# The order of the Strassen slots of the first feed-forward network, on TensorE, ScalarE and VectorE

## The chip, the cores and the metric

One core of a Trainium2 chip runs the whole program in one launch. The metric is the device time of that core in microseconds; the kernel before takes 1050.8 us (median of three runs, 1050.67 to 1052.14). TensorE multiplies, ScalarE (ACT) applies functions and copies, VectorE (DVE) and GpSimd (POOL) do elementwise work, SyncE (SP) issues most DMAs.

## The reference

A channel attention over 6016 tokens of 256 channels is followed by two feed-forward networks (256 to 2048 to 256), in float32:

```python
x = attn_out.reshape(B * S, D)
h = x @ w_in;   x = (h * np.cos(h)) @ w_out                 # first network ("FFN 1")
h = x @ w_in2;  x = (h * (1 / (1 + np.exp(-h)))) @ w_out2   # second ("FFN 2")
```

The kernel folds the attention matrix into the first network's weights, so that this network's input is v.

## The kernel before

The 6016 tokens are cut into 12 blocks: 11 of 512 columns and a last ("plain") one of 384. Each block passes the 2048 hidden features in eight steps of two times 128 (`NPAIR`). One such pair of one block is a *slot*. Every float32 operand is kept as a high and a low part (`hi`, a rounded copy, and `lo`, the remainder), and each product is three matmuls (`PASSES`): high by high, low weight by high, high by low.

From block 3 on, the first layer of FFN 1 is formed by seven Strassen products P1 to P7 on quarter blocks (`product`, L974; 256 columns each) instead of eight plain ones. Blocks 3 to 10 make 64 such slots, numbered 0 to 7 here within a block by the pair; the plain block's eight follow, and then FFN 2 with 88 Strassen slots of its own.

`first_layer` (L1325) writes out one step of a software pipeline by hand; each engine runs its instructions in the order in which this function issues them. Step j works on three units: u (slot j, whose products begin), p (slot j-1, whose products end, and whose cosines are taken) and q (slot j-2, whose result enters the output matmuls). For u, P1 goes into x2 (`xz[k2][:, 1]`), P7 on z2 (`xz[k2][:, 0]`); ScalarE copies z2 aside (`p7s`, L1346) and x2 into y2 (`ys[k2][:, 1]`, L1350); P2 is added onto x2, P6 onto y2, and y2 is copied aside as u2 (L1403). One step later, for p: P4 is added onto z and VectorE adds u2 (L1335; the addition itself is in `add`, L1028); P5 onto y, and VectorE adds the P7 copy into `ys[k][:, 0]` (L1361); P3 onto y. Then `xz` and `ys` hold the four quarters of the hidden block. Each of the two goes through a sine on ScalarE (L1348 for xz, L1386 for ys; a cosine by its bias), a multiply of the two on VectorE (L1362, L1390), the high part on ScalarE (L1374 "hi1", L1391 "hi0") and the low part on VectorE (L1375 "lo1", L1400 "lo0"). The 12 output matmuls of 512 columns (`o1_of`, L1304, matmul at L1315) run as 2, 6 and 4 between the products.

Beside this chain the slots carry *side work* for later stages, placed by the slot's number in `misc_act`, `misc_dve` and `misc_late` (L1233 to L1262):
- the next block's V: four GpSimd subtractions ("V forms"), its high parts on ScalarE (L923, L927) and low parts on GpSimd (L916), in slots 1, 2, 3; the reduction of its largest values on VectorE (L401) in slot 3; its bound, two small matmuls and two small VectorE steps, in slot 7;
- the decoding of FFN 2's weights in phases: a ScalarE copy (L313) with a GpSimd step (L290) in slots 5 and 7, two VectorE "clamps" (L296, L297) in slots 6 and 0, a VectorE sign step (L303) with GpSimd's L306 and combine (L355) in slots 7 and 1, and the split, a ScalarE copy (L358) with two GpSimd subtractions (L360), in slots 0 and 3;
- x2, the previous block's input to FFN 2 (`begin_x2`, L826): three copies out of the outputs in slot 4, the forms on VectorE (L858, L861) and GpSimd (L862), high parts on ScalarE (L848) and low parts on GpSimd (L853) in slots 5, 6, 7, each low followed by two stores on SP's queue.

In the kernel before, all of a slot's side work stands between the P7 copy and hi1 in program order. A slot ends with

```python
            product(y2, "P6", w_, x_, start=False)      # L1396
            nc.scalar.activation(u2, y2, AF.Copy)       # L1403
```

## Time and profile before

| | |
|---|---|
| median of 3 runs | 1050.8 us |
| the profiled execution's own time | 1052.19 us |
| its span, first to last instruction | 1050.3 us |
| TensorE busy | 1006.4 us (96%) |
| VectorE busy | 857.5 us (82%) |
| ScalarE busy | 796.7 us (76%) |
| GpSimd busy | 371.7 us (35%) |
| granted TensorE clock, mean | 0.999 |
| idle of TensorE before the outputs' L1315, put down to hi0 (L1391) | 17.0 us |

Busy time is the share in which an engine has an instruction running; matmuls are pipelined and their recorded lengths overlap the next ones' starts, so a TensorE that reads as busy need not be issuing as fast as it can. The chain that ended last gives 57% of the span to TensorE, 18% to ScalarE and 14% to VectorE. Times in rows are microseconds from the start of the span; L numbers are lines of the kernel before.

### The profile page before, as it was taken

To read this page: it belongs to the slowest core of one execution; us is meant where nothing else is said; L and a number is where in the kernel's file an instruction comes from. 1 tells how busy PE (TensorE), PEld (TensorE's weight loads), DVE (VectorE), ACT (ScalarE), POOL (GpSimd) and SP (SyncE) were. 2 spreads that over 40 slices of the span, in tenths; PEclk is the share of its full clock that TensorE was granted. 3 is DMA by queue.
4 is the path that set the end of the run, shared out by engine and by line. 5 is a ranking of instruction groups with operands and counts; after the bars stand their busy time and mean duration, and the time that the engine had idled before them with its cause. 6 is when DMAs were issued, how large, how long until landed. Compare 5 with 4: busy or idle time off the path is not lost.

```text
span 1050.3 us, 18664 instructions
## 1 busy us (share of the span) xinstructions
PE 1006.4 (96%) x7062; PEld 935.5 (89%) x7062; DVE 857.5 (82%) x1295; ACT 796.7 (76%) x1453; POOL 371.7 (35%) x367
## 2 busy tenths in 40 slices
PE   9999999999999898999989999999999999999998
PEld 8767888888888787888878999999999999999997
DVE  6799889777767777777877589999999999999972
ACT  6786676677777777777777688888878888888863
POOL 4433388526456464646435311111111111111110
PEclk9999999999999999999999999999999999999999
DMA  9940036422333333243336971202211220220101
GB/s 349 347 154 1 1 139 239 163 90 106 126 120 131 111 121 131 81 151 116 129 132 244 413 290 71 91 11 82 91 57 46 81 91 12 81 91 12 56 22 38
DMA packets 35012, 126.59 MB, mean 121 GB/s; under 512 B 3170, under 2 KB 4450, under 8 KB 30178
## 3 DMA queue, kind: packets, MB, share of 16 engines
q1 hardware_dynamic: 34770, 125.12, 32.2%
q8 instruction: 57, 0.93, 0.4%
q14 instruction: 41, 0.34, 0.1%
q10 hardware_dynamic: 144, 0.20, 0.1%
HBM read 73.01 MB, written 52.30 MB: 119 GB/s over the span
## 4 chain that ended last, share of the span: by engine, by line
PE 57%; ACT 18%; DVE 14%; issue 7%; DMA 2%; POOL 1%; SPq 0%; DVEq 0%; ACTq 0%; POOLq 0%
PE o L978 19%; PE xz L978 12%; PE ys L978 9%; PE o L766 6%; DVE ys L1390 4%; PE h L734 3%; ACT hi L1391 3%; ACT t L1348 3%; ACT hi L1374 3%; DVE xz L1028 3%; ACT t L1386 2%; DVE lo L1375 2%; ACT ys L1350 2%; DMA qk<-qk_dram 2%; PE o L1018 1%
## 5 line engine op out<-in xcount | busy, mean ns | idle before, releaser
L796 DVE TENSOR_TENSOR lo<-t,hi 128x768 fp32r<-128x768 f32 (+1 forms) x176 | 194.8, 1116 | 28.7 <-ACT hi L788 28.5
L783 POOL TENSOR_TENSOR t<-t 128x256 f32<-128x256 f32 x88 | 64.5, 733 | 356.7 <-DVE t L780 296.7
L788 ACT ACTIVATE hi<-t 128x768 fp32r<-128x768 f32 (+1 forms) x176 | 169.1, 961 | 27.2 <-PE o L978 26.2
L1315 PE MATMUL o<-hi,wo 128*128 128x512 f32 x512 | 137.4, 391 | 18.0 <-ACT hi L1391 17.0
L978 PE MATMUL o<-hi,wo 128*128 128x256 f32 x770 | 134.6, 275 | 0.0
L1315 PEld LDWEIGHTS o<-hi,wo 128*128 128x128 f32 x512 | 87.0, 189 | 35.6 <-ACT hi L1391 28.8
L978 PEld LDWEIGHTS o<-hi,wo 128*128 128x128 f32 x770 | 116.9, 192 | 0.0
L978 PE MATMUL o<-lo,wo 128*128 128x256 f32 x385 | 105.9, 275 | 0.0
L978 PE MATMUL xz<-xhi,wa 128*128 128x256 f32 x384 | 77.8, 288 | 12.5 <-DVE lo L1375 10.3
L1391 ACT ACTIVATE hi<-ys 128x512 fp32r<-128x512 f32 x64 | 38.2, 597 | 57.1 <-DVE ys L1390 57.1
L978 PEld LDWEIGHTS xz<-xhi,wa 128*128 128x128 f32 x384 | 62.6, 190 | 20.6 <-DVE lo L1375 12.5
L1400 DVE TENSOR_TENSOR lo<-ys,hi 128x512 fp32r<-128x512 f32 x64 | 44.3, 692 | 40.3 <-ACT hi L1391 40.3
L978 PE MATMUL ys<-xhi,wf 128*128 128x256 f32 x384 | 74.0, 274 | 0.5 <-DVE ys L1028 0.5
L978 PEld LDWEIGHTS ys<-xhi,wf 128*128 128x128 f32 x384 | 67.7, 190 | 7.5 <-DVE ys L1028 0.7
L978 PEld LDWEIGHTS o<-lo,wo 128*128 128x128 f32 x385 | 73.9, 192 | 0.0
L1348 ACT ACTIVATE t<-xz,half_pi,smalls 128x512 f32<-128x512 f32 x64 | 49.8, 778 | 31.3 <-DVE xz L1028 30.9
L1467 ACT ACTIVATE ys<-xz 128x256 f32<-128x256 f32 x88 | 32.4, 368 | 45.4 <-PE xz L978 44.5
L1315 PE MATMUL o<-lo,wo 128*128 128x512 f32 x256 | 65.9, 380 | 0.0
L978 PE MATMUL xz<-x2hi,wf 128*128 128x256 f32 x352 | 65.8, 275 | 0.0
L978 PE MATMUL xz<-x2hi,wa 128*128 128x256 f32 x352 | 65.8, 275 | 0.0
L766 PE MATMUL o<-hi,wo 128*128 128x512 f32 (+1 forms) x256 | 62.7, 367 | 1.4 <-POOL wo L351 1.4
L1375 DVE TENSOR_TENSOR lo<-xz,hi 128x512 fp32r<-128x512 f32 x64 | 44.1, 689 | 24.4 <-ACT hi L1374 23.7
(271 smaller groups left out, 3176.8 us busy)
## 6 DMA issues: line engine op xcount, KB each, us to landing
qk<-qk_dram SPq DMA_DIRECT2D x22, 512.0 KB, 7.6
x2hi<-xshi SPq DMA_DIRECT2D x11, 896.0 KB, 5.3
x2lo<-xslo SPq DMA_DIRECT2D x11, 896.0 KB, 7.2
wi_dram<-stage SPq DMA_DIRECT2D x8, 1024.0 KB, 4.4
wo_dram<-stage SPq DMA_DIRECT2D x8, 1024.0 KB, 4.7
vraw<-vT_dram SPq DMA_DIRECT2D x11, 512.0 KB, 5.8
outT_dram<-q SPq DMA_DIRECT2D x22, 256.0 KB, 2.0
xshi<-t SPq DMA_DIRECT2D x10, 512.0 KB, 2.6
```

The source lines that it names most:

```text
L766: nc.tensor.matmul(o[:, e, :n], wo1_at(i, f)[:, e * P : (e + 1) * P], columns(parts[k][:, s, :n]), start=(f == 0 and (i, k) == PASSES[0]), ...
L783: eng.tensor_tensor(out=t[:, 7, :c], in0=t[:, 3, :c], in1=t[:, 6, :c], op=ALU.subtract)
L788: nc.scalar.activation(hi[:, sl, :c], t[:, 1:][:, sl, :c], AF.Copy)
L796: nc.vector.tensor_tensor(out=lo[:, sl, :c], in0=t[:, 1:][:, sl, :c], in1=hi[:, sl, :c].bitcast(F32), op=ALU.subtract)
L978: nc.tensor.matmul(out, w(p, ka), columns(x[r][:, kb - 1]), start=(start and i == 0), stop=(stop and i == 2), skip_group_check=True,)
L1315: nc.tensor.matmul(o[:, e], wo1_at(i, f)[:, e * P : (e + 1) * P], columns(parts[k][:, s]), start=(f == 0 and (i, k) == PASSES[0]), stop=(f ...
L1348: nc.scalar.activation(sines[:, 1], xz[k], AF.Sin, bias=half_pi, scale=small[p[1]])
L1375: nc.vector.tensor_tensor(out=ls[:, 1], in0=xz[k], in1=hs[:, 1].bitcast(F32), op=ALU.subtract)
L1390: nc.vector.tensor_tensor(out=ys[k], in0=ys[k], in1=sines[:, 0], op=ALU.mult)
L1391: nc.scalar.activation(hs[:, 0], ys[k], AF.Copy)
L1400: nc.vector.tensor_tensor(out=ls[:, 0], in0=ys[k], in1=hs[:, 0].bitcast(F32), op=ALU.subtract)
L1467: nc.scalar.activation(y2, x2, AF.Copy)
```

## The change

The slot keeps its products, copies, sines, multiplies and parts; their order and the place of the side work are others.
- TensorE: P4 and P5 of p come first, then P1 and P7 of u, then P3 between two pairs of output matmuls, P6 in mid slot, and P2 last, behind the remaining four pairs. Outputs run from separate lists of high and low passes, two matmuls at a time.
- ScalarE: the y2 copy first, then the two sines one after the other, the P7 copy, hi1, hi0, u2; `misc_act` follows u2.
- VectorE: the two additions, `misc_dve`, the two multiplies, lo1, lo0, then the bound and `misc_late`.
- One buffer for the P7 copy (`seeds[0]`) where two took turns; x2's third seed is always `seeds[2]`.
- x2's steps are the same four for every block: the raw low parts now stand a slot later than the raw high parts.
- When the last Strassen slot's outputs meet the plain block, they are spread over two steps (`halved`).

```diff
@@ -828,8 +828,6 @@
         if b == PLAIN:
             return begin_x2_plain(b)
         c, t, t0 = HB, Y, seeds[2]
-        if FIRST <= b < PLAIN - 1:
-            t0 = plain_part(T[1])[:, :HB]
         src = [state[1, b][:, a].rearrange("p (b h j) -> p j h b", h=2, j=2) for a in range(CH)]
         nc.scalar.activation(t[:, 1:3].rearrange("p j (h b) -> p j h b", h=2), src[1], AF.Copy)
         nc.scalar.activation(t0.rearrange("p (h b) -> p h b", h=2), src[0][:, 0], AF.Copy)
@@ -867,17 +865,10 @@
                 lambda: (low("raw", RAW), high("formed", FORMED)),
                 lambda: low("formed", FORMED),
             ]
-        if b < 2:
-            return [
-                lambda: forms(nc.vector, eng),
-                lambda: high("raw", RAW),
-                lambda: (low("raw", RAW), high("formed", FORMED)),
-                lambda: low("formed", FORMED),
-            ]
         return [
             lambda: forms(nc.vector, eng),
-            lambda: (high("raw", RAW), low("raw", RAW)),
-            lambda: high("formed", FORMED),
+            lambda: high("raw", RAW),
+            lambda: (low("raw", RAW), high("formed", FORMED)),
             lambda: low("formed", FORMED),
         ]
 
@@ -1239,6 +1230,8 @@
             xsteps[1]()
         if m in (6, 7):
             xsteps[m - 4]()
+        if m == 7:
+            xsteps.clear()
         decode_steps(b, m, "act")
         if b + 1 < PLAIN:
             if m == 1:
@@ -1252,8 +1245,6 @@
         decode_steps(b, m, "dve")
         if m == 5:
             xsteps[0]()
-        if m == 7:
-            xsteps.clear()
         if b + 1 == PLAIN and m == 2:
             vs.pop(0)()
 
@@ -1306,10 +1297,11 @@
         if (1, b) not in state:
             state[1, b] = ps_o.tile([P, CH, TB], F32, tag="o", name=f"o1_{b}")
         o = state[1, b]
-        todo = [(s, r, e) for r in PASSES for s in range(2) for e in range(CH)]
-
-        def run(count):
-            for _ in range(count):
+        high = [(s, r, e) for r in PASSES[:2] for s in range(2) for e in range(CH)]
+        low = [(s, PASSES[2], e) for s in range(2) for e in range(CH)]
+
+        def run(todo):
+            for _ in range(CH):
                 s, (i, k), e = todo.pop(0)
                 f = 2 * m + s
                 nc.tensor.matmul(
@@ -1318,20 +1310,30 @@
                     columns(parts[k][:, s]),
                     start=(f == 0 and (i, k) == PASSES[0]),
                     stop=(f == NF - 1 and (i, k) == PASSES[-1]),
+                    skip_group_check=True,
                 )
 
-        return run
+        return lambda: run(high), lambda: run(low)
+
+    halved = []
 
     def first_layer(j, u, p, q, o):
         k, k2 = (j - 1) % 2, j % 2
         up, pp_, qp, op_ = [v is not None and v[1] == PLAIN for v in (u, p, q, o)]
         ps, qs = p is not None and not pp_, q is not None and not qp
-        p7s, u2 = seeds[::2], seeds[1]
+        p7, u2 = seeds[:2]
+        o_high = o_low = lambda: None
+        if qs:
+            o_high, o_low = o1_of(q[1:], hl.pop(j - 2))
+        if qs and pp_:
+            halved.extend([o_high, o_high, o_high, o_high, o_low, o_low])
+            o_high = o_low = lambda: None
         if ps:
             w, x = w1_slot(p[2]), xparts[p[:2]]
             y, z = ys[k][:, 1], xz[k][:, 0]
             sines, hs, ls = [parted(r) for r in (T[0], HI[k], LO[k])]
             product(z, "P4", w, x, start=False)
+            product(y, "P5", w, x, start=False)
             add(z, z, u2)
         if j < 2:
             open_quadrants(j)
@@ -1343,64 +1345,61 @@
             y2, x2, z2 = ys[k2][:, 1], xz[k2][:, 1], xz[k2][:, 0]
             product(x2, "P1", w_, x_, start=True)
             product(z2, "P7", w_, x_, start=False)
-            nc.scalar.activation(p7s[k2], z2, AF.Copy)
+        if ps:
+            add(ys[k][:, 0], y, p7)
+        if not up:
+            misc_dve(u[1], u[2])
+            nc.scalar.activation(y2, x2, AF.Copy)
+        o_high()
         if ps:
             nc.scalar.activation(sines[:, 1], xz[k], AF.Sin, bias=half_pi, scale=small[p[1]])
+            product(y, "P3", w, x, start=False)
+            nc.scalar.activation(sines[:, 0], ys[k], AF.Sin, bias=half_pi, scale=small[p[1]])
         if not up:
-            nc.scalar.activation(y2, x2, AF.Copy)
+            nc.scalar.activation(p7, z2, AF.Copy)
+        if ps:
+            nc.vector.tensor_tensor(out=xz[k], in0=xz[k], in1=sines[:, 1], op=ALU.mult)
+            nc.scalar.activation(hs[:, 1], xz[k], AF.Copy)
+            nc.vector.tensor_tensor(out=ys[k], in0=ys[k], in1=sines[:, 0], op=ALU.mult)
+            nc.scalar.activation(hs[:, 0], ys[k], AF.Copy)
+            for i, r in ((1, xz[k]), (0, ys[k])):
+                nc.vector.tensor_tensor(out=ls[:, i], in0=r, in1=hs[:, i].bitcast(F32), op=ALU.subtract)
+            hl[j - 1] = [flat(r[k]) for r in (HI, LO)]
         if j < 2:
             step()
         if j == 0:
             parts[pend] = emit_split(pend, units[pend])
         while left and (j == 1 or len(left) > 2):
             emit_left()
-        if qs and not qp:
-            hl.setdefault(("run", j - 2), o1_of(q[1:], hl.pop(j - 2)))(2)
-        if ps:
-            product(y, "P5", w, x, start=False)
-            add(ys[k][:, 0], y, p7s[k])
-            nc.vector.tensor_tensor(out=xz[k], in0=xz[k], in1=sines[:, 1], op=ALU.mult)
+        o_high()
+        if not up:
+            product(y2, "P6", w_, x_, start=False)
+        o_low()
+        o_high()
+        o_high()
+        o_low()
         if pp_:
             plain_cosines(j - 1, p)
         if qp:
             high_and_low(j - 2, q, True)
         if up:
             tail_of_first(j)
-        else:
-            misc_act(u[1], u[2])
-            misc_dve(u[1], u[2])
-            misc_late(u[1], u[2])
-        if ps:
-            nc.scalar.activation(hs[:, 1], xz[k], AF.Copy)
-            nc.vector.tensor_tensor(out=ls[:, 1], in0=xz[k], in1=hs[:, 1].bitcast(F32), op=ALU.subtract)
         if qp:
             high_and_low(j - 2, q, False)
-        if qs:
-            hl["run", j - 2](6 if ps else 4)
+        if halved:
+            for _ in range(3):
+                halved.pop(0)()
         elif op_:
             emit_o1(o[1:], hl.pop(j - LAG2))
-        elif ("run", j - LAG2) in hl:
-            hl.pop(("run", j - LAG2))(6)
-        if ps:
-            product(y, "P3", w, x, start=False)
-            nc.scalar.activation(sines[:, 0], ys[k], AF.Sin, bias=half_pi, scale=small[p[1]])
-        if qs and ps:
-            hl.pop(("run", j - 2))(4)
-        if ps:
-            nc.vector.tensor_tensor(out=ys[k], in0=ys[k], in1=sines[:, 0], op=ALU.mult)
-            nc.scalar.activation(hs[:, 0], ys[k], AF.Copy)
         if up:
             emit_plain_h1(u[1:], 1, bank(ys[k2], BLOCKS[PLAIN][1]))
         else:
+            nc.scalar.activation(u2, y2, AF.Copy)
             product(x2, "P2", w_, x_, start=False)
-            product(y2, "P6", w_, x_, start=False)
             if u[2] == NPAIR - 1:
                 bound(u[1] + 1, xz[k][:, 0])
-        if ps:
-            nc.vector.tensor_tensor(out=ls[:, 0], in0=ys[k], in1=hs[:, 0].bitcast(F32), op=ALU.subtract)
-            hl[j - 1] = [flat(r[k]) for r in (HI, LO)]
-        if not up:
-            nc.scalar.activation(u2, y2, AF.Copy)
+            misc_act(u[1], u[2])
+            misc_late(u[1], u[2])
 
     def tail_of_first(j):
         nonlocal q_sums, late
```

How this moves instructions: a middle slot on TensorE, before (xz_1463 and ys_1462 belong to p, xz_1423 to u; wa and wf are weights, o the outputs):

```order
L978 MATMUL xz_1463<-xhi_1152,wa_90 128x256 x2
L978 MATMUL xz_1463<-xlo_1153,wa_90 128x256
L978 MATMUL xz_1423<-xhi_1152,wa_91 128x256 x2
L978 MATMUL xz_1423<-xlo_1153,wa_91 128x256
L978 MATMUL xz_1423<-xhi_1152,wf_1049 128x256 x2
L978 MATMUL xz_1423<-xlo_1153,wf_1049 128x256
L1315 MATMUL o_3_1528<-hi_502,wo_1_94 128x512 x2
L978 MATMUL ys_1462<-xhi_1152,wf_1048 128x256 x2
L978 MATMUL ys_1462<-xlo_1153,wf_1048 128x256
L1315 MATMUL o_3_1528<-hi_502,wo_1_94 128x512 x6
L978 MATMUL ys_1462<-xhi_1152,wf_1048 128x256 x2
L978 MATMUL ys_1462<-xlo_1153,wf_1048 128x256
```

and in the change (xz_1466 and ys_1465 belong to p, xz_1423 and ys_1422 to u):

```order
L969 MATMUL xz_1466<-xhi_1152,wa_90 128x256 x2
L969 MATMUL xz_1466<-xlo_1153,wa_90 128x256
L969 MATMUL ys_1465<-xhi_1152,wf_1048 128x256 x2
L969 MATMUL ys_1465<-xlo_1153,wf_1048 128x256
L969 MATMUL xz_1423<-xhi_1152,wa_91 128x256 x2
L969 MATMUL xz_1423<-xlo_1153,wa_91 128x256
L969 MATMUL xz_1423<-xhi_1152,wf_1049 128x256 x2
L969 MATMUL xz_1423<-xlo_1153,wf_1049 128x256
L1307 MATMUL o_3_1515<-hi_502,wo_1_94 128x512 x2
L969 MATMUL ys_1465<-xhi_1152,wf_1048 128x256 x2
L969 MATMUL ys_1465<-xlo_1153,wf_1048 128x256
L1307 MATMUL o_3_1515<-hi_502,wo_1_94 128x512 x2
```

P5 (the first two rows of ys before) has moved up to the place behind P4, ahead of P1 and P7, and only two output matmuls stand ahead of P3.

ScalarE in slot 2 of a block, before (spare and p are the two P7 copies, t the sines, u is u2):

```order
L1346 ACTIVATE p_1053<-xz_1423 128x256
L1348 ACTIVATE t_500<-xz_1463,half_pi,smalls 128x2x256
L1350 ACTIVATE ys_1422<-xz_1423 128x256
L927 ACTIVATE xhi_2794<-vform_2796 128x1024
L1374 ACTIVATE hi_503<-xz_1463 128x2x256
L1386 ACTIVATE t_500<-ys_1462,half_pi,smalls 128x2x256
L1391 ACTIVATE hi_503<-ys_1462 128x2x256
L1403 ACTIVATE u_1054<-ys_1422 128x256
```

and in the change:

```order
L1352 ACTIVATE ys_1422<-xz_1423 128x256
L1355 ACTIVATE t_500<-xz_1466,half_pi,smalls 128x2x256
L1357 ACTIVATE t_500<-ys_1465,half_pi,smalls 128x2x256
L1359 ACTIVATE p_1053<-xz_1423 128x256
L1362 ACTIVATE hi_503<-xz_1466 128x2x256
L1364 ACTIVATE hi_503<-ys_1465 128x2x256
L1397 ACTIVATE u_1054<-ys_1422 128x256
L918 ACTIVATE xhi_2828<-vform_2830 128x1024
```

The copy xhi<-vform, side work of slot 2, stood ahead of the high parts hi and now stands behind u2, ahead of the next slot's y2 copy; the sines t stand together.

GpSimd in slots 0 to 2 of a block, before (stage is the split, vform the V forms, xlo V's low part):

```order
L360 TENSOR_TENSOR stage<-wv_wi_2575,stage 128x512 x2
L916 TENSOR_TENSOR vform_2796<-vraw_2518 128x256 x2
L916 TENSOR_TENSOR vform_2796<-vraw_2518,vform_2796 128x256 x2
L306 TENSOR_TENSOR wv_wi_2680<-wv_wi_2680,raw_wi_2366 128x512
L355 TENSOR_TENSOR wv_wi_2680<-wv_wi_2680 128x128 x4
L916 TENSOR_TENSOR xlo_2795<-vraw_2518,xhi_2794 128x768
```

and in the change:

```order
L360 TENSOR_TENSOR stage<-wv_wi_2601,stage 128x512 x2
L306 TENSOR_TENSOR wv_wi_2718<-wv_wi_2718,raw_wi_2352 128x512
L355 TENSOR_TENSOR wv_wi_2718<-wv_wi_2718 128x128 x4
L907 TENSOR_TENSOR vform_2830<-vraw_2544 128x256 x2
L907 TENSOR_TENSOR vform_2830<-vraw_2544,vform_2830 128x256 x2
L907 TENSOR_TENSOR xlo_2829<-vraw_2544,xhi_2828 128x768
```

The sign step and combine of slot 1 (wv_wi, L306 and L355) have moved ahead of the four V forms.

## Rows read from the trace of the kernel before

**Rows 1.** Stretch of FFN 1's slots, busy us: PE, PEld, DVE, ACT, POOL; clock, DMA.
```profile
350.00:400.00 50.00, 45.79 (x288) 40.91 (x288) 37.60 (x63) 37.97 (x73) 28.76 (x30) 1.00 0.31 111
```

**Rows 2.** Line L1403, u2's copy, one a slot: durations, first and last start.
```profile
L1403 ACT ACTIVATE u<-ys x64: 378/379/383, 194.6 to 562.5; 128x256 f32<-128x256 f32 x64
```

**Rows 3.** Line L1512, the same copy in FFN 2's Strassen slots.
```profile
L1512 ACT ACTIVATE u<-ys x88: 380/406/428, 597.5 to 1005.3; 128x256 f32<-128x256 f32 x88
```

**Rows 4.** Timeline, TensorE, block 6: start, length, instruction, count, idle before, releaser.
```profile
364.57 0.49 PE L978 MATMUL xz<-xhi,wa 128*128 128x256 f32 x2 [1.24 <-DVE lo L1375]
...
364.90 0.28 PE L978 MATMUL xz<-xlo,wa 128*128 128x256 f32 x1
...
366.68 1.46 PE L1315 MATMUL o<-hi,wo 128*128 128x512 f32 x6
...
368.31 1.03 PE L1315 MATMUL o<-lo,wo 128*128 128x512 f32 x4
...
371.45 0.70 PE L1315 MATMUL o<-hi,wo 128*128 128x512 f32 x2 [0.37 <-ACT hi L1391]
```

**Rows 5.** Timeline, ScalarE, blocks 3 to 7.
```profile
202.28 0.38 ACT L1403 ACTIVATE u<-ys 128x256 f32<-128x256 f32 x1
...
360.82 0.83 ACT L848 ACTIVATE hi<-y 128x768 fp32r<-128x768 f32 x1
...
361.55 0.83 ACT L313 ACTIVATE wv_wi<-raw_wi 128x512 f32<-128x512 f32 x1
...
366.86 0.78 ACT L1348 ACTIVATE t<-xz,half_pi,smalls 128x512 f32<-128x512 f32 x1 [0.55 <-DVE xz L1028]
...
367.53 0.37 ACT L1350 ACTIVATE ys<-xz 128x256 f32<-128x256 f32 x1
...
368.78 0.59 ACT L1374 ACTIVATE hi<-xz 128x512 fp32r<-128x512 f32 x1
...
378.88 1.05 ACT L358 ACTIVATE stage<-wv_wi 128x1024 fp32r<-128x1024 f32 x1
...
390.32 1.04 ACT L927 ACTIVATE xhi<-vform 128x1024 fp32r<-128x1024 f32 x1
```

**Rows 6.** VectorE: timeline of one slot; then line L401, the reduction, all of them.
```profile
366.40 0.42 DVE L1028 TENSOR_TENSOR xz<-xz,u 128x256 f32<-128x256 f32 x1
...
367.66 0.70 DVE L1362 TENSOR_TENSOR xz<-xz,t 128x512 f32<-128x512 f32 x1 [0.35 <-ACT t L1348]
...
368.27 0.42 DVE L296 TENSOR_SCALAR wv_wi<-wv_wi 128x512 f32<-128x512 f32 x1
...
369.39 0.69 DVE L1375 TENSOR_TENSOR lo<-xz,hi 128x512 fp32r<-128x512 f32 x1 [0.24 <-ACT hi L1374]
...
L401 DVE TENSOR_REDUCE most<-vraw x10: 944/1207/1210, 139.1 to 535.7; 128x8 bf16<-128x1024 f32 x9, 128x6 bf16<-128x768 f32 x1
```

**Rows 7.** Timeline, GpSimd steps and the VectorE steps under them.
```profile
361.73 1.91 POOL L853 TENSOR_TENSOR lo<-y,hi 128x768 fp32r<-128x768 f32 x1 [6.17 <-ACT hi L848]
...
362.05 1.87 DVE L861 TENSOR_TENSOR y<-y 128x256 f32<-128x256 f32 x1
...
565.53 2.73 POOL L360 TENSOR_TENSOR stage<-wv_wo,stage 128x512 fp32r<-128x512 f32 x2 [1.58 <-ACT stage L358]
...
565.74 1.38 DVE L297 TENSOR_SCALAR wv_wo<-wv_wo 128x512 int32<-128x512 int32 x1
```

**Rows 8.** Timeline, GpSimd, slots 0 and 1 of block 7.
```profile
380.01 2.57 POOL L360 TENSOR_TENSOR stage<-wv_wi,stage 128x512 fp32r<-128x512 f32 x2 [1.91 <-ACT stage L358]
382.65 1.66 POOL L916 TENSOR_TENSOR vform<-vraw 128x256 f32<-128x256 f32 x2
384.39 2.02 POOL L916 TENSOR_TENSOR vform<-vraw,vform 128x256 f32<-128x256 f32 x2
386.36 1.30 POOL L306 TENSOR_TENSOR wv_wi<-wv_wi,raw_wi 128x512 int32<-128x512 int32 x1
387.74 1.94 POOL L355 TENSOR_TENSOR wv_wi<-wv_wi 128x128 f32<-128x128 f32 x4
```

## The prediction, made before the changed kernel was run

> **What bounds the kernel now.** I read the page's busy shares first: TensorE carries most of the span. Then the stretches: in the middle of the first feed-forward network's Strassen slots TensorE is busy 45.8 of 50 us with the granted clock at 1.00, while VectorE has 37.6 and ScalarE 38.0 [rows 1]. So no engine is full there; the time is in waits between them. The 64 slots run from 194.6 to 562.5 us, counted by the copy u2 that ends each [rows 2]; the first interval is 7.64 [rows 5], so the other 62 take 360.2, **5.81 us a slot, 46.5 a block** of eight.
>
> How fast could a slot be? The second network shows TensorE without such waits: 87 slots of 42 matmuls of 256 columns in 407.8 us [rows 3] is 4.69 a slot and 0.1116 a matmul. A matmul of 512 columns is (1.46 - 1.03)/2 = 0.215 [rows 4]. A slot of the first network has seven products of three matmuls and 12 output matmuls: 21 x 0.1116 + 12 x 0.215 = **4.92 us**. The 0.89 between is lost at places such as those in [rows 4]: the output matmuls wait 0.37 for ScalarE's last high part, and in slot 5 P1 waits 1.24 for a low part on VectorE. The old order needs hi0 early in a slot, and between u2 and hi0 lie two trips to VectorE and back, with the side copies between them.
>
> **The new order, one plain slot.** Time 0 is P4's first matmul. TensorE, if nothing holds it: P4 to 0.34, P5 0.67, P1 1.01, P7 1.34, an output pair 1.77, P3 2.11, a pair 2.54, P6 2.87, four pairs 4.59, P2 4.92. A product's result is there about 0.2 after its last matmul is issued away (a matmul lasts 0.28 [rows 4] against 0.11 to issue, and a wait takes 0.03 to 0.04 to wake: an add ends at 366.82, its sine starts at 366.86 [rows 5, 6]). ScalarE starts the next instruction 0.11 before the last ends (0.67 for a sine of 0.78 [rows 5]), VectorE 0.09 (0.61 for a multiply of 0.70 [rows 6]).
> - VectorE: add z 0.54 to 0.96, add y 0.87 to 1.30. P3 needs this at 1.77: spare 0.47.
> - ScalarE: the copy y2 reads the tile that P7 still writes, so I hold it behind P7: 1.54. First sine 1.80 to 2.58; second sine waits for P3, but ScalarE is free only at 2.47: to 3.25; p7's copy at 3.14.
> - VectorE: multiply xz 2.62 to 3.32, multiply ys 3.29 to 3.99.
> - ScalarE: hi1 3.42, hi0 4.03, u2 4.52 to 4.90. The next slot's P5, at 4.92 + 0.34 = 5.26, needs u2: **spare 0.32**.
> - VectorE: lo1 4.05 to 4.74, lo0 4.66 to 5.35; P1 of the next slot, at 5.60, needs lo1.
>
> So in a plain slot nothing holds TensorE, and it takes its 4.92. Output matmuls use parts of the slot before and never wait. What leaves the path: the wait for hi0 ahead of the outputs, and side copies between a sine and a high part. What gets a new place on it: P5 is now second in the slot and waits for u2, so P1, P7 and everything behind queue behind u2.
>
> The Trainium skill, "PSUM — Partial Sum Buffer", section "PSUM bank collisions raise a hardware error", says that accesses are to be guarded by bank, not by address, which speaks for holding y2 behind P7 and not P1. No row of before shows which of the two y2 waits for. Behind P1 it would be ready 0.34 earlier; the slot would still be TensorE's 4.92.
>
> **The side work.** Between u2 and the next y2 ScalarE has room from 4.79 to 6.46, 1.67 us. The side copies are 1.05, 1.04 and, most in one slot, two of 0.83 [rows 5]: all fit, at no cost. VectorE has room between add y (1.21) and multiply xz (2.62), 1.4 us: the two clamps, 0.42 each [rows 6], the sign step and the forms fit. Four things don't fit:
> 1. Slot 3's reduction of the next V block, 1.21 [rows 6], now follows lo0: 5.26 to 6.47. Slot 4's add z starts at 1.46 instead of 0.54, add y ends 2.22, P3 starts 2.25 instead of 1.77: **+0.5**.
> 2. GpSimd. In slot 1 its sign and combine steps now precede the four V forms. Slot 0's split copy ends 0.9 into slot 1; then 2.64 + 1.38 + 1.94 + 1.74 + 1.97, start to start or length [rows 8], ends the forms 10.6 into slot 1, 0.7 into slot 3. The copy of those forms at the end of slot 2 waits for this, hands ScalarE on at 1.7 against 1.54, and delays item 1 further: **+0.1**.
> 3. VectorE's side steps that read and write SBUF stall under a running GpSimd step. L861 took 1.87 with L853 on GpSimd from before its start, and L297 1.38 under L360, where its like L296 takes 0.42 [rows 6, 7]; each ended about 0.3 after GpSimd's. With the new places, clamps of slots 0 and 6 meet GpSimd's low parts (begun 0.4 into slot 0, when L306 and L355, 3.3 together [rows 8], have followed slot 7's sign step at about 2.0; and 0.7 into slot 6, behind a high part of 0.83 that starts at 4.79 in slot 5). Multiply xz moves from 2.62 to about 3.2 in each, 0.5 beyond which u2's spare covers 0.3: **+0.2 each, 0.4**. L861 itself, in slot 5, is freed: its GpSimd neighbour moves to slot 6.
> 4. A wait that is met late exposes about 0.1 of weight load (a pair of output matmuls takes 0.70 after a wait [rows 4]; unwaited it would be 0.215 + 0.38, where 0.38 = 1.46 - 5 x 0.215). For the five slots above and the block change: **+0.5**.
>
> A block: 8 x 4.92 + 0.5 + 0.1 + 0.4 + 0.5 = **40.9**, 5.11 a slot. Bounds: 39.4 with no item, and 46.5 if everything gained at TensorE returns as waits. I take 40.9, since only few places per block have less spare than their side work.
>
> Edits with no cost: one p7 buffer instead of two (p7's copy at 3.14 follows its reader, add y, at 1.30); the third seed buffer in place of a piece of T; the split raw steps of x2, whose stores leave GpSimd a slot later and are read only in the second network; the outputs spread over the two plain slots at the end (same 12 matmuls). On SP's queue those stores come a slot later, and slot 4's load of V half a slot later, for a use five slots on; nothing else moves past another there. From slot 64 on the program is as before, TensorE stays full, and the 43 us arrive at the end.
>
> **The sum.** 62 x (5.81 - 5.11) = 43.4; I leave slot 1 at its 7.6. Profiled span 1050.3 - 43.4 = 1006.9, with the 1.9 us around it 1008.8; the profiled execution (1052.19) was 1.4 above the median, so against the median of 1050.8 it is 1007.4. I say **1008**.
>
> **Rivals.**
> - *ScalarE's head of the slot becomes the bound.* Three side copies a block (slots 0, 2 and 3) wait for GpSimd and now stand in front of y2, with the whole chain behind them. For it: GpSimd's row of steps in slots 0 to 2 leaves item 2 only 0.1. Against: GpSimd is busy only 28.8 of 50 us [rows 1], so a backlog clears within the block. If each is 1.5 us late past its room: 40.9 + 4.5 = 45.4 a block, 1050.8 - 7.75 x 1.1 = 1042. Chance 0.12, for 1024 to 1046.
> - *Slower: the stall under GpSimd.* Eight VectorE side steps a block (four clamps, two forms, two sign steps) move to a place between two chained steps. If each stalls as L861 did, 1.87 - 0.42 = 1.45 [rows 6, 7], that is 11.6; the spare of 0.32 in five slots hides 1.6, and 0.4 is in the sum already: 40.9 + 9.6 = 50.5, so 1050.8 + 7.75 x 4.0 = 1082. It decides from about five of the eight: 5 x 1.45 = 7.25 less 2.0 is 5.3, against the 5.6 gained. For it: L861 and L297. Against: GpSimd is idle 21 of 50 us [rows 1], so the eight can't all meet it. The Trainium skill, "SBUF — State Buffer", section "SBUF: two separate sides", has this as a rule: one port pair shared by VectorE and GpSimd, held for a whole instruction, the other side "fully blocks". By that rule each overlap costs the rest of GpSimd's step, and the traced 1.87 and 1.38 agree. Chance 0.05.
> - *Better than the walk*: items 1 to 4 hidden in the spares: 39.4 a block, 1050.8 - 7.75 x 7.1 = 996. Chance 0.06 below 999.
> - *The second network's weights.* Their fetches start in slot 59; six Strassen slots pass them 4 us sooner. If TensorE then waits for them, 4 us come back: 1012, inside the range.
>
> **How the numbers follow.** Forecast (999 to 1024) 0.77, ScalarE's head 0.12, the stall 0.05, better 0.06. The range 998 to 1026 takes in the walk's bounds and the mildest part of the first rival. A measurement here tells 0.2% (2 us) from no change. Faster by more: the forecast's 0.77, the better case's 0.06 and 0.10 of the first rival, 0.93 together; the other 0.02 of that rival is no change, and the stall's 0.05 is slower.
>
> **What would show it.** Right: u2's copies 4.9 to 5.1 apart in most slots, slot 4 the longest at 5.4 to 5.8; TensorE busy over 48.5 of 50 in the stage; the output matmuls' wait for a high part gone from the waits; the form L861 near 0.42; a few P5 or P3 waits left, below 0.5 each. Wrong: the ScalarE copies of V forms or weights waiting over 1 us for GpSimd with TensorE idle behind u2; clamps of 1.4 us in most slots; slots of 5.5 without a named wait, which would mean that the chain from u2 round to u2 is longer than 4.6 (4.92 - 0.32).

## The result and the profile after

The changed kernel takes **1008.95 us** (median of four runs, 1008.56 to 1009.99) against 1051.12 us of the kernel before on the same chip: ratio 0.960, 95% interval 0.958 to 0.962. A second session gave 1008.25 us and 0.959 (0.958 to 0.960). The profiled execution took 1008.56 us, its span 1006.4; the granted clock is 0.999 as before. The forecast was 1008.

The page of the changed kernel, its busy times and two groups of instructions:

```profile
PE 988.8 (98%) x7062; PEld 927.4 (92%) x7062; DVE 855.4 (85%) x1295; ACT 796.3 (79%) x1453; POOL 376.0 (37%) x367
...
L1307 PE MATMUL o<-hi,wo 128*128 128x512 f32 x512 | 142.0, 380 | 0.0
...
L969 PE MATMUL ys<-xhi,wf 128*128 128x256 f32 x384 | 77.5, 284 | 4.8 <-DVE ys L1019 3.6
```

The instructions are the same in number and the work of VectorE and ScalarE in length. TensorE's idle time fell from 43.9 us to 17.6, and its recorded busy time fell by 17.6 as well: a wait that the recorded length of a matmul covers counts as busy. The output matmuls (L1307) have no idle time ahead of them, where the table of before had 17.0 us; 4.8 us of idle time, 0.5 before, now stand ahead of TensorE's products into ys (P5, P3 and P6).

The same stretch as [rows 1], a little further on in the work:

```profile
350.00:400.00 50.00, 49.31 (x323) 45.03 (x322) 42.23 (x73) 41.90 (x81) 33.01 (x35) 1.00 0.40 138
```

TensorE is busy 49.3 of 50 us and has 323 recorded matmuls, not 288. The copy u2 and its like in the second network answer to [rows 2, 3]:

```profile
L1397 ACT ACTIVATE u<-ys x64: 373/380/390, 193.3 to 518.3; 128x256 f32<-128x256 f32 x64
```
```profile
L1511 ACT ACTIVATE u<-ys x88: 383/406/425, 553.8 to 961.5; 128x256 f32<-128x256 f32 x88
```

The first copy is at 193.29 (194.64 before), the second at 198.60, the last at 518.25. So the 62 slots between take 319.65 us, **5.156 a slot, 41.25 a block**, 40.6 us less than the 360.2 of before. The first interval fell from 7.64 to 5.31 (2.3 us) and the stage starts 1.35 earlier. From the last slot to the second network's first copy it is 35.55, before 34.98: 0.6 is given back in the plain slots. The second network takes 407.7 against 407.8. The sum, 40.6 + 2.3 + 1.35 - 0.6 = 43.7, is the difference of the spans, 43.9, to 0.2. The 1.35 is not shown to be the change's: after_again (below), the same kernel, has its first copy at 192.56, and eight_outputs, which is the same up to there, at 196.22, while the profiled execution of before was 1.4 above its median. Without it the sum is 42.3, and the medians are 42.2 apart.

**The ring.** ScalarE in the changed kernel, from slot 2's side copy to slot 4's y2 copy (timeline: start, length, instruction, idle before):

```profile
328.73 1.07 ACT L918 ACTIVATE xhi<-vform 128x1024 fp32r<-128x1024 f32 x1 [1.11 <-POOL vform L907]
329.71 0.37 ACT L1352 ACTIVATE ys<-xz 128x256 f32<-128x256 f32 x1
330.01 0.76 ACT L1355 ACTIVATE t<-xz,half_pi,smalls 128x512 f32<-128x512 f32 x1
330.67 0.77 ACT L1357 ACTIVATE t<-ys,half_pi,smalls 128x512 f32<-128x512 f32 x1
331.33 0.38 ACT L1359 ACTIVATE p<-xz 128x256 f32<-128x256 f32 x1
331.60 0.60 ACT L1362 ACTIVATE hi<-xz 128x512 fp32r<-128x512 f32 x1
332.21 0.60 ACT L1364 ACTIVATE hi<-ys 128x512 fp32r<-128x512 f32 x1
332.70 0.38 ACT L1397 ACTIVATE u<-ys 128x256 f32<-128x256 f32 x1
332.97 1.06 ACT L358 ACTIVATE stage<-wv_wi 128x1024 fp32r<-128x1024 f32 x1
334.44 0.37 ACT L1352 ACTIVATE ys<-xz 128x256 f32<-128x256 f32 x1 [0.42 <-PE xz L969]
```

From y2's copy to the end of u2 ScalarE runs without a gap. TensorE's P5 waits for u2 (it starts at 333.14, next rows), P1 and P7 follow, and the next y2 copy waits for P7: it starts at 334.44, 4.73 after the last. That chain, from y2's copy back to y2's copy, is what I call the ring. It closes in 4.73 us, against TensorE's 4.92: 3.37 to the end of u2, 0.06 to P5, 1.30 to the next y2. The side copy L358 ends at 334.03 and hides in it; L918, which started 1.11 late, doesn't.

**The two other places**, TensorE and VectorE behind that slot (P4's last row, P5, P7's last row, an output pair, P3):

```profile
332.86 0.28 PE L969 MATMUL xz<-xlo,wa 128*128 128x256 f32 x1
333.14 0.49 PE L969 MATMUL ys<-xhi,wf 128*128 128x256 f32 x2
...
334.13 0.28 PE L969 MATMUL xz<-xlo,wf 128*128 128x256 f32 x1
334.24 0.60 PE L1307 MATMUL o<-hi,wo 128*128 128x512 f32 x2
335.38 0.49 PE L969 MATMUL ys<-xhi,wf 128*128 128x256 f32 x2 [0.54 <-DVE ys L1019]
```
```profile
333.45 1.21 DVE L401 TENSOR_REDUCE most<-vraw 128x8 bf16<-128x1024 f32 x1
334.58 0.42 DVE L1019 TENSOR_TENSOR xz<-xz,u 128x256 f32<-128x256 f32 x1
334.91 0.42 DVE L1019 TENSOR_TENSOR ys<-ys,p 128x256 f32<-128x256 f32 x1
```

P5 at 333.14 would have started at 332.86 + 0.11 = 332.97: 0.17 late, and its first two matmuls take 0.49 where unwaited pairs take 0.39: 0.10 of weight load. P3 at 335.38 would have been at 334.24 + 0.43 = 334.67: 0.71 late and 0.11 more, because slot 3's reduction held the two additions back.

The 0.10 of weight load at P5 is in the ring's 4.73, since P5 came late. One slot earlier nothing held P5 up (u2's copy on ScalarE, P5 on TensorE):

```profile
327.23 0.39 ACT L1397 ACTIVATE u<-ys 128x256 f32<-128x256 f32 x1
```
```profile
327.98 0.39 PE L969 MATMUL ys<-xhi,wf 128*128 128x256 f32 x2
```

u2 ends at 327.62 and P5 starts in its turn, 0.36 later. A P5 that waits starts 0.06 behind u2, so u2 had 0.30 to spare here.

Side steps that meet, VectorE and GpSimd in slots 6 and 0 (two answers of the timeline):

```profile
344.98 1.50 DVE L296 TENSOR_SCALAR wv_wi<-wv_wi 128x512 f32<-128x512 f32 x1
...
355.92 1.39 DVE L297 TENSOR_SCALAR wv_wi<-wv_wi 128x512 int32<-128x512 int32 x1
...
360.45 0.81 DVE L303 SCALAR_TENSOR_TENSOR wv_wi<-raw_wi,wv_wi 128x512 int32<-128x512 int32 x1
```
```profile
344.37 1.83 POOL L851 TENSOR_TENSOR lo<-y,hi 128x768 fp32r<-128x768 f32 x1 [1.37 <-ACT hi L846]
...
354.33 2.69 POOL L851 TENSOR_TENSOR t<-y,t 128x512 fp32r<-128x512 f32 x2
...
360.45 3.18 POOL L360 TENSOR_TENSOR stage<-wv_wi,stage 128x512 fp32r<-128x512 f32 x2 [2.39 <-ACT stage L358]
```

A clamp of 0.42 that starts under GpSimd's L851 ends 0.28 to 0.29 after it (344.37 + 1.83 = 346.20, clamp to 346.48; 357.02, clamp to 357.31), as in [rows 7]. The P5s behind these two slots are late by 0.26 + 0.10 and 0.22 + 0.11, read as above.

### The profile page after: what moved, and what is told of

Read it like the earlier page. It is cut to its first block, busy times and chain, and to the rows that moved or that the text cites. A ratio compares the mean times of both kernels' runs of the same rounds, so it can differ in the third digit from the quotient of the medians.

```text
span 1006.4 us, 18716 instructions
## 1 busy us (share of the span) xinstructions
PE 988.8 (98%) x7062; PEld 927.4 (92%) x7062; DVE 855.4 (85%) x1295; ACT 796.3 (79%) x1453; POOL 376.0 (37%) x367
## 4 chain that ended last, share of the span: by engine, by line
PE 72%; DVE 9%; ACT 8%; DMA 5%; POOL 3%; issue 3%; SPq 0%; ACTq 0%; DVEq 0%; POOLq 0%
PE o L969 20%; PE xz L969 15%; PE ys L969 12%; PE o L766 6%; PE o L1307 6%; PE h L734 4%; DMA vraw<-vT_dram 3%; ACT hi L1362 2%; PE o L1009 2%; DMA qk<-qk_dram 2%; PE S L539 1%; POOL stage L360 1%; ACT t L1357 1%; ACT u L1397 1%; DVE lo L1366 1%
## 5 line engine op out<-in xcount | busy, mean ns | idle before, releaser
L1307 PE MATMUL o<-hi,wo 128*128 128x512 f32 x512 | 142.0, 380 | 0.0
L1307 PEld LDWEIGHTS o<-hi,wo 128*128 128x128 f32 x512 | 87.4, 191 | 6.8
L969 PE MATMUL ys<-xhi,wf 128*128 128x256 f32 x384 | 77.5, 284 | 4.8 <-DVE ys L1019 3.6
L1361 DVE TENSOR_TENSOR xz<-xz,t 128x512 f32<-128x512 f32 x64 | 44.6, 697 | 37.7 <-ACT t L1355 36.9
L1307 PE MATMUL o<-lo,wo 128*128 128x512 f32 x256 | 76.1, 380 | 0.0
L969 PE MATMUL xz<-xhi,wa 128*128 128x256 f32 x384 | 72.0, 277 | 0.0
L775 DVE TENSOR_TENSOR t<-t 128x512 f32<-128x512 f32 x88 | 60.2, 684 | 0.2 <-ACT t L1509 0.2
L1496 ACT ACTIVATE t<-t 128x512 f32<-128x512 f32 x88 | 55.6, 632 | 2.2 <-DVE t L1019 2.1
L969 PE MATMUL o<-hi,late 128*128 128x256 f32 x308 | 53.9, 275 | 0.0
```

What stands on the lines that cost most here:

```text
L775: eng.tensor_tensor(out=t[:, 4:6, :c], in0=t[:, 0:1, :c].to_broadcast([P, 2, c]), in1=t[:, 1:3, :c], op=ALU.subtract)
L969: nc.tensor.matmul(out, w(p, ka), columns(x[r][:, kb - 1]), start=(start and i == 0), stop=(stop and i == 2), skip_group_check=True,)
L1307: nc.tensor.matmul(o[:, e], wo1_at(i, f)[:, e * P : (e + 1) * P], columns(parts[k][:, s]), start=(f == 0 and (i, k) == PASSES[0]), stop=(f ...
L1361: nc.vector.tensor_tensor(out=xz[k], in0=xz[k], in1=sines[:, 1], op=ALU.mult)
L1496: nc.scalar.activation(t[:, 0:2], t[:, 0:2], AF.Silu)
```

## The experiments

Ratios are to the kernel before, of the same session; a slot is the mean interval of the 62 u2 copies, (last start - second start)/62.

| run | us | ratio, 95% interval | a slot |
|---|---|---|---|
| the change | 1008.95 | 0.9599 (0.9582 to 0.9616) | 5.156 |
| after_again | 1008.25 | 0.9591 (0.9578 to 0.9604) | 5.155 |
| sines_apart | 1080.28 | 1.0278 (1.0248 to 1.0308) | 6.283 |
| side_before_hi1 | 1045.7 | 0.9952 (0.9929 to 0.9974) | 5.747 |
| p6_last | 1025.73 | 0.9759 (0.9730 to 0.9787) | 5.427 |
| old_order_side_last | 1064.38 | 1.0124 (1.0107 to 1.0140) | 6.001 |
| eight_outputs | 1005.36 | 0.9565 (0.9535 to 0.9595) | 5.103 |
| reduce_in_slot4 | 1002.74 | 0.9536 (0.9523 to 0.9550) | 5.060 |
| forms_first | 1000.83 | 0.9519 (0.9506 to 0.9532) | 5.035 |
| clamps_early | 1003.0 | 0.9544 (0.9528 to 0.9560) | 5.062 |
| p5_third | 1016.03 | 0.9667 (0.9654 to 0.9680) | 5.255 |
| reduce_and_p5 | 1009.51 | 0.9601 (0.9588 to 0.9614) | 5.149 |
| all_and_p5 | 1004.2 | 0.9545 (0.9532 to 0.9558) | 5.074 |

after_again is the changed kernel once more, beside variants of it:

> The changed kernel itself, as the measure for the three beside it on the same chip: 1008 to 1010 us.

**Which part of the order matters.** Three kernels undo one part of the change each.

sines_apart puts the second sine behind hi1 again:

```diff
-            nc.scalar.activation(sines[:, 0], ys[k], AF.Sin, ...)
...
             nc.scalar.activation(hs[:, 1], xz[k], AF.Copy)
+            nc.scalar.activation(sines[:, 0], ys[k], AF.Sin, ...)
```

> The new order, but the second sine stands behind hi1, as in the old order. Theory (a ring from u2 round to u2 that just fits under TensorE's 4.92 us a slot, spare 0.32): hi1 waits for multiply xz and starts at 3.36, the second sine at 3.85 instead of 2.47, multiply ys at 4.67, hi0 at 5.41, u2 at 5.90 to 6.28; the next P5, due at 5.26, waits about 1.05 us in every slot. Slots of 6.0 us, about 1071 us in all (1055 to 1085), slower than the old order; TensorE's wait stands at P5 for u2. Rival (the gain comes from the matmul order alone, ScalarE has idle time for any order): within 5 us of the changed kernel's 1009.

It took 1080.28, inside the range and slower than the kernel before. Its waits on TensorE (total, times, longest) put it on P5:

```profile
PE ys L969 <- ACT u L1397: 52.0, 55, 1.7
```

ScalarE's trips to VectorE show in its timeline, hi1 waiting for one multiply and hi0 for the other:

```profile
349.61 0.60 ACT L1361 ACTIVATE hi<-xz 128x512 fp32r<-128x512 f32 x1 [0.85 <-DVE xz L1360]
...
351.65 0.60 ACT L1364 ACTIVATE hi<-ys 128x512 fp32r<-128x512 f32 x1 [0.77 <-DVE ys L1363]
```

With both sines ahead of hi1, the second sine and the P7 copy cover the first multiply, and hi1 covers the second.

side_before_hi1 puts ScalarE's side work ahead of hi1 again:

```diff
             nc.scalar.activation(p7, z2, AF.Copy)
+            misc_act(u[1], u[2])
...
-            misc_act(u[1], u[2])
             misc_late(u[1], u[2])
```

> The new order, but ScalarE's side copies stand between the P7 copy and hi1 again. Theory: a slot's 0.75 to 1.4 us of side copies go into the ring ahead of hi0 and u2; hi0 starts at 4.5 to 5.2 instead of 4.03, u2 is 0.5 to 1.2 later against a spare of 0.32, so P5 waits 0.3 to 0.9 in each slot: 5.4 to 5.7 us a slot, 1022 to 1045 us in all, likeliest 1034. Rival (the place of the side work costs nothing, since ScalarE is busy 42 of 50 us in either order): within 5 us of 1009.

1045.7: the direction held, the size was more than expected, 0.7 past the range. A side copy is then part of the ring in its slot, and P5 waits for u2 in most slots:

```profile
PE ys L969 <- ACT u L1398: 23.3, 53, 0.9
```

p6_last puts P6 behind P2 and u2 behind both:

```diff
-            product(y2, "P6", w_, x_, start=False)
...
-            nc.scalar.activation(u2, y2, AF.Copy)
             product(x2, "P2", w_, x_, start=False)
+            product(y2, "P6", w_, x_, start=False)
+            nc.scalar.activation(u2, y2, AF.Copy)
```

> The new order, but P6 stands behind P2 at the slot's end, and u2's copy behind it. Theory: P6's result is there at 4.92 + 0.2 = 5.12, u2 at 5.12 to 5.50, visible at 5.54, while the next P5 is due at 5.26: it waits about 0.28 and exposes 0.1 of weight load in every plain slot; slots where the ring was late anyway gain nothing more. About 5.3 us a slot, 1009 + 62 x 0.25 = 1024 us (1016 to 1032). Rival (P6's place is free, u2's copy hides behind the next slot's P4): 1007 to 1012.

1025.73, as expected. The losses of the three, 71, 37 and 17 us, add to 125, where the whole change brought 42: the parts don't add. Each one, undone by itself, makes the ring longer than TensorE's 4.92 (slots of 6.08, 5.5 and 5.40), and with P5 second in the slot TensorE then waits for it in nearly all; the order before, where P5 comes later, did not pay that. Not undone by themselves are VectorE's order, the two lists of output matmuls, the single P7 buffer and x2's steps, so no run shows what each of these gives.

old_order_side_last is the other half of the question, the kernel before with the late side work alone moved, ScalarE's and, with `misc_late`, VectorE's reduction too:

```diff
-            misc_act(u[1], u[2])
             misc_dve(u[1], u[2])
-            misc_late(u[1], u[2])
...
             nc.scalar.activation(u2, y2, AF.Copy)
+            misc_act(u[1], u[2])
+            misc_late(u[1], u[2])
```

> The kernel before with one part of the change alone: the old order of a slot, but ScalarE's side work (the decode's and the split's copies) issued behind u2's copy instead of ahead of the first high part's copy. Theory (the order of the sines and of P2/P6 is what the 43 us came from, and the side copies only have to be out of the way of the copy that the new order waits for): in the old order a copy behind u2 stands ahead of P7's copy and the first sine of the next slot, which TensorE waits for just the same, so little is won: 1045 to 1060 us. Rival (the place of the side work is the gain, the order is not): most of the 43 us comes here, 1010 to 1025.

1064.38, slower than before by 1.2% (1.1 to 1.4), 4 us above the range. The rival is out. TensorE's waits in the slots (total, times, longest), first of the kernel before, then of this one:

```profile
PE o L1315 <- ACT hi L1391: 16.7, 47, 0.4
PEld xz L978 <- DVE lo L1375: 12.0, 11, 1.4
```
```profile
PE o L1315 <- ACT hi L1389: 17.4, 53, 0.4
PEld xz L978 <- DVE lo L1373: 20.1, 39, 0.9
PEld ys L978 <- DVE ys L1028: 4.5, 8, 0.6
```

(PEld is the queue of weight loads.) The outputs' wait for hi0 stays as it was. P1's weights wait for a low part 39 times, where they did 11 times, 8.1 us more, and once a block the addition to y comes late, as it does in the change behind the reduction; it had cost 0.7 us in all before. The two are about the 62 x 0.19 = 12 us that the slots grew. The run moved both engines' work, so it does not tell what ScalarE's copies cost by themselves.

**How long is the ring?** eight_outputs leaves out the four low-part output matmuls of a slot, 4 x 0.215 = 0.86 us of TensorE:

```diff
-                    stop=(f == NF - 1 and (i, k) == PASSES[-1]),
+                    stop=(f == NF - 1 and (i, k) == PASSES[1]),
...
-        return lambda: run(high), lambda: run(low)
+        return lambda: run(high), lambda: None
```

> Leaves out of each Strassen slot of the first network the four output matmuls that take the low part (8 of 12 run; nothing else changes). TensorE has 4 x 0.215 = 0.86 us less to issue per slot. Theory: the ring is 4.92 - 0.32 = 4.60 us, so a plain slot falls to 4.6 and no further, and every side step that was hidden by the spare now adds in full: 39 to 39.8 us a block instead of 41.4, 990 to 998 us in all. Rival (TensorE's issue is the only bound, the ring has ample slack): 8 x 0.86 = 6.9 a block, 62 x 0.86 = 53 us less, 956 us (950 to 965).

It gained 3.6 us where 11 to 19 were expected. Its u2 intervals by slot (0 to 7, each the time from the copy before; medians over the blocks, as in what follows) are 5.64, 4.73, 4.72, 5.65, 5.40, 4.72, 5.51, 4.72: those without late side work show the ring of 4.72, and TensorE waits in nearly all:

```profile
PE ys L969 <- ACT u L1397: 30.0, 54, 1.2
```

The expectation took 4.92 - 0.32 = 4.60 for the ring. But where TensorE waits for u2 in each slot, each slot also pays P5's 0.10 of weight load, and the ring is 4.73: 62 x 0.13 = 8 of the 7 to 15 us by which the run missed its range. Ring plus side work is 41.1 a block (the sum of the eight), where the changed kernel's medians come to 41.5. TensorE's own rate and the ring are nearly the same bound now.

**What the late side work costs.** reduce_in_slot4 moves the reduction from the end of slot 3 to VectorE's room in slot 4, behind the additions:

```diff
     def misc_dve(b, m):
         decode_steps(b, m, "dve")
+        if m == 4:
+            span_of(b + 1, raws.pop(b + 1))
...
     def misc_late(b, m):
-        if m == 3:
-            span_of(b + 1, raws.pop(b + 1))
+        pass
```

> The new order, but the reduction of the next V block (1.21 us on VectorE) stands in slot 4 between add y and multiply xz, not behind slot 3's lo0. Theory: the profile of the change shows TensorE waiting at slot 4's P3 for add y, 0.71 us and 0.11 of exposed load in each of seven to eight blocks; VectorE's room there is 1.4 us, so the wait goes and nothing takes its place: 8 x 0.8 = 6 us less, 1003 us (1002 to 1005). Rival (the late low parts or the multiplies become the wait, since VectorE is busy 42 of 50 us): 1007 to 1011.

1002.74, as expected: slot 4 falls from 5.41 to 4.72, and no wait of TensorE for L1019 is left.

forms_first has that and one more step moved, a sign step with the GpSimd work behind it:

```diff
-        "dve": {..., 0: [(1, 1, 1)], 1: [(1, 1, 2)]},
+        "dve": {..., 0: [(1, 1, 1)], 2: [(1, 1, 2)]},
```

> reduce_in_slot4 with one more step moved: VectorE's sign and clamp step of the second decode goes from slot 1 to slot 2, so that GpSimd's operations that follow it no longer stand ahead of V's forms on GpSimd's queue. Theory (slot 3 is long because ScalarE's copy L918 waits for those forms, and u2 of the next slot behind it): slot 3 falls from 5.45 to about 4.95, 0.5 per block, so about 999 us (996 to 1002). Rival (slot 3 is long for its own side copies on ScalarE, however early the forms are): 1002 to 1004. Rival (the moved step lands under other GpSimd work and is stretched): over 1004.

1000.83, the fastest here. GpSimd's forms now precede the sign step, and ScalarE's copy of them doesn't wait (L918 had 1.11 in the changed kernel):

```profile
320.15 2.04 POOL L907 TENSOR_TENSOR vform<-vraw,vform 128x256 f32<-128x256 f32 x2
322.15 1.30 POOL L306 TENSOR_TENSOR wv_wi<-wv_wi,raw_wi 128x512 int32<-128x512 int32 x1
```
```profile
324.31 1.06 ACT L918 ACTIVATE xhi<-vform 128x1024 fp32r<-128x1024 f32 x1
```

Slot 3 falls from 5.44 (reduce_in_slot4) to 4.93 as expected, but slot 4 rises from 4.72 to 4.94, TensorE's own time: a slot behind a late one had been short because u2 caught up. So 0.3 a block is left, 2 us; the two intervals of the ratio overlap, and it is the slots that show the step, not the time.

clamps_early also puts the first decode a slot earlier, so that its clamps run in slot 5, ahead of GpSimd's step:

```diff
-        "act": {5: [(0, 0, 0)], ...},   "dve": {6: [(0, 0, 1)], ...},
+        "act": {4: [(0, 0, 0)], ...},   "dve": {5: [(0, 0, 1)], ...},
```

with the forms split so that only the first of them, L856, precedes the clamps.

> forms_first with the first decode of a block one slot earlier: ScalarE's part in slot 4 instead of 5, VectorE's clamps in slot 5, between the first of x2's forms and the others, where GpSimd has not begun. Theory (the clamp that is stretched to 1.5 us under GpSimd in slot 6 makes the add to z and y and so a sine late): slot 6 falls from 5.5 to about 4.95, another 0.5 per block, about 995 us (991 to 999). Rival (slot 6 is long for ScalarE's two copies of x2's high part, which stay): the time of forms_first within 2 us. Rival (slot 5 grows by what slot 6 loses): the same or slower.

The third case came: slot 6 falls from 5.50 to 4.72 and slot 5 rises from 4.94 to 5.80. Slot 6's excess over TensorE's 4.93 went with the clamps; that it is now shorter still is the catching up behind a late slot. (ScalarE's decode copy left slot 5 too, but in the changed kernel it had not held y2 up: it ends at 344.95, P7 at 345.09, and y2 starts at 345.12, while hi1 waits 0.46 for the multiply behind the clamps.) VectorE's slot 5:

```profile
336.74 1.25 DVE L856 TENSOR_TENSOR y<-spare,y 128x512 f32<-128x512 f32 x1
337.92 0.41 DVE L296 TENSOR_SCALAR wv_wi<-wv_wi 128x512 f32<-128x512 f32 x1
338.37 0.43 DVE L297 TENSOR_SCALAR wv_wi<-wv_wi 128x512 int32<-128x512 int32 x1
338.71 0.42 DVE L861 TENSOR_TENSOR y<-y 128x256 f32<-128x256 f32 x1
339.05 0.69 DVE L1372 TENSOR_TENSOR xz<-xz,t 128x512 f32<-128x512 f32 x1
```

and GpSimd's step beside it:

```profile
336.57 0.90 POOL L290 TENSOR_SCALAR raw_wi<-raw_wi 128x512 int32<-128x512 uint32 x1
```

The clamps are free at 0.41 and 0.43, but GpSimd's L290, which follows ScalarE's part of the decode, came a slot earlier too, and the form L856 takes 1.25 beside it (0.68 in the changed kernel). So 2.3 us stand between the additions and the multiply, where a plain slot has room for 1.4. That GpSimd had not begun there was wrong.

**P5 behind P1**, a try to give u2 more room, missed:

```diff
-            product(y, "P5", w, x, start=False)
...
             product(x2, "P1", w_, x_, start=True)
-            product(z2, "P7", w_, x_, start=False)
         if ps:
+            product(y, "P5", w, x, start=False)
             add(ys[k][:, 0], y, p7)
         if not up:
+            product(z2, "P7", w_, x_, start=False)
```

> The new order, but TensorE issues P4, P1, P5, P7 instead of P4, P5, P1, P7. Theory: P5 needs u2, P1 doesn't, so u2's spare grows by one product, 0.34, to 0.66; the profile of the change shows P5 late by 0.17, 0.26 and 0.22 in three slots of a block, each with 0.1 of exposed load, and these 0.96 go; add y comes 0.34 later and P3's spare falls from 0.47 to 0.13, so slot 4's wait at P3, 0.71, grows by about 0.3. Net 0.6 a block, 5 us less, 1004 us (1002 to 1007). Rival (P3 becomes the wait in every slot, its spare being used up): 1009 to 1018.

1016.03. The interval of slot 0 is 6.78, where it was 5.65. At a block's change P1 waits until VectorE has worked out the new block's bound in the tile that P1 writes (L432, by the start times), and P5 now queues behind P1 (TensorE: P4's last, P1, P5; then VectorE):

```profile
357.02 0.28 PE L969 MATMUL xz<-xlo,wa 128*128 128x256 f32 x1
357.36 0.49 PE L969 MATMUL xz<-xhi,wa 128*128 128x256 f32 x2
357.69 0.28 PE L969 MATMUL xz<-xlo,wa 128*128 128x256 f32 x1
357.80 0.39 PE L969 MATMUL ys<-xhi,wf 128*128 128x256 f32 x2
```
```profile
357.15 0.16 DVE L432 TENSOR_SCALAR smalls<-xz 128x1 f32<-128x1 f32 x1
...
358.33 0.43 DVE L1019 TENSOR_TENSOR ys<-ys,p 128x256 f32<-128x256 f32 x1 [0.50 <-PE ys L969]
358.67 1.54 DVE L296 TENSOR_SCALAR wv_wi<-wv_wi 128x512 f32<-128x512 f32 x1
360.25 1.02 DVE L297 TENSOR_SCALAR wv_wi<-wv_wi 128x512 int32<-128x512 int32 x1
```

Behind P4, P5 would have started at 357.13; it starts at 357.80. The addition to y and the clamps move back with it, and the clamps take 2.6 us there (to 361.27), 2.1 in the changed kernel (355.24 to 357.31). The two, 0.67 and 0.5, are about the 1.13 by which the slot grew. With slot 3's reduction moved as well, and P5 still third:

> Both edits: the reduction in slot 4's room and P5 as third product. Theory: all named waits of TensorE go, 0.82 + 0.96 = 1.8 a block; slots close to 4.92 us, 39.6 to 40 a block, 62 x 0.2 = 13 us less than the change: 996 us (994 to 1000). Rival (the two are not additive, as slot 4's room is then too short with add y 0.34 later): 1000 to 1005.

1009.51, a miss by the same slot (6.78). all_and_p5 is clamps_early with P5 third except where P1 waits:

```diff
+            early = up or u[2] == 0
+            if early:
+                product(y, "P5", w, x, start=False)
...
+            if ps and not early:
+                product(y, "P5", w, x, start=False)
```

> clamps_early with P5 behind P1 instead of ahead of it, except in the slot after a block's change, where P1 itself waits for VectorE's low part (the wait that made p5_third slow there: 0.71 us on L1367). Theory (p5_third failed by that one slot, in the others P5 no longer waits for u2): about 0.3 to 0.5 per block less than clamps_early, 991 to 993. Rival (P3 behind it loses its spare and waits for the add to y in every slot, as p5_third's 15.1 us in 57 waits say): the same as clamps_early or up to 5 us slower.

1004.2, the ratio of clamps_early: the rival. (Its expectation lays p5_third's slot 0 to P1's wait for a low part, 0.71 us; that wait comes a slot later, and the rows above show where the lateness begins.) P5 no longer waits for u2 in most slots, but P3 waits for the addition to y behind P5, on the queue of weight loads:

```profile
PEld ys L977 <- DVE ys L1027: 8.7, 55, 0.2
```

## Why the prediction was right, and where it wasn't

- **What bounds it**: right. The wait for hi0 is gone from the outputs, TensorE is busy 49.3 of 50 us, and the second network takes what it did.
- **The walk of a plain slot**: right in its order, and in its size where nothing holds TensorE: 4.93 against 4.92, a spare of 0.30 against 0.32. What holds y2 is P7, as held, at P7's end (334.13 + 0.28 = 334.41, y2 at 334.44). That is what the Trainium skill, "PSUM — Partial Sum Buffer", section "PSUM bank collisions raise a hardware error", spoke for; no run here has a y2 that could start behind P1. What the last sign of the prediction had wrong is the "4.6" for a ring that TensorE waits for: it is 4.73, as the late P5 adds its 0.10 of weight load to it.
- **Side item 1**, slot 3's reduction: forecast 0.5 with 0.1 of weight load, read 0.71 + 0.11; undoing it gave (5.156 - 5.060) x 8 = 0.77 a block. Shown. This is the term that was most mis-sized, and through item 2: the reduction starts at 333.45, 0.82 behind P4 (332.63), where the walk had 0.34. Of these 0.48, P3 is itself put off by the 0.27 of the late P5; the other 0.21 are 0.71 less 0.5.
- **Item 2**, the late forms: forecast 0.1, read 0.17 + 0.10 at P5, and the 0.21 of item 1. The forms end 1.05 into slot 3 (328.69, P4 at 327.64), not 0.7; one of the steps ahead of them, L360, takes 3.18 beside VectorE's L303, where [rows 8] had 2.57, a stall that the prediction had in the other direction only. forms_first shows that GpSimd's order is the cause.
- **Item 3**, clamps under GpSimd: forecast 0.2 each in slots 6 and 0, read 0.26 and 0.22. For slot 6 clamps_early shows it; slot 0's was not tried alone. The form L861, now L859, is free as forecast (median 0.425, 1.87 before).
- **Item 4**, 0.1 at each late wait: read 0.10 to 0.11 at four of them, 0.42 against 0.5.
- **The block**: 40.9 forecast, 41.25 measured. The items come to 1.8 instead of 1.5, and the plain slot's 4.93 instead of 4.92 is the rest. So 62 slots gave 40.6 and not 43.4.
- **What made the sum come out**: luck, in part. The slots gave 2.8 less than forecast, and 1.7 that the sum left out make up for more than half of it: 2.3 in slot 1 (left at 7.6, measured 5.31) less 0.6 in the plain slots. The order of the slot gives the 2.3, as old_order_side_last keeps 7.64; by which wait, no run shows, and the cause of the 0.6 is open too.
- **The signs**: u2's intervals by slot are 5.65, 4.72, 4.93, 5.47, 5.41, 5.06, 5.50 and 4.72, not 4.9 to 5.1 in most with slot 4 the longest. Behind a slot whose u2 is late the next interval is short, so only the two together tell what TensorE lost. P3's wait, 0.71, is above the 0.5 that was named.
- **The rivals**: ScalarE's head of the slot is there, but in slot 2 alone, where L918 waits for GpSimd by up to 1.1 us and P5 loses the 0.27. The stall under GpSimd took place in two of eight side steps (1.50 and 1.39), and by 0.23 in a third (L296 of slot 0, 0.65), not in the five from which it decides. The Trainium skill's page "SBUF — State Buffer", section "SBUF: two separate sides", says of such an overlap that the side that comes second waits for the other's whole instruction, and the traced 1.50 and 1.39 agree; how many overlaps occur is a matter of the places. No wait for the second network's weights appeared: its 88 slots take what they did.

## What to carry to other kernels

Where engines pass a chain round from one step to the next, find the ring (the operation that waits for its own successor a step earlier), add it up by start times, and put it against the fullest engine's own issue time: work taken from one of the two counts only until the other is the longer one, as eight_outputs shows: 0.86 us a slot taken from TensorE gave 3.6 us in all. Side work goes where the ring has its wait, and its cost is read from the slots that are longer than the others together with the short ones behind them, each undone by itself. Moving it costs what the new place has too little of, as slot 5 of clamps_early did.

## What was not expected of the hardware

The stall between VectorE and GpSimd goes both ways: GpSimd's pair L360 takes 3.18 us where VectorE's sign step L303 starts with it (360.45 both) and 2.52 where none does (forms_first, at 315.81). In the one block of the changed kernel where L360 started 0.10 before L303 (401.91, 402.01), L303 took 1.78 instead of 0.81. In the same stretches VectorE's low parts (L1366), which read one operand from PSUM, keep their 0.69 us. A held VectorE step ends later behind GpSimd's the longer it is itself: the clamps, 0.42 alone, end 0.28 to 0.29 after it, the form L856, 0.68 alone, 0.52 after it (clamps_early).
